# Attention kernel on one core: values loaded 128 rows at a time, odd key spans filled by copies, block sums from the loaded rows, and a new order of the attention stage

## The chip, the core and the metric

The program runs on one core of a Trainium2 chip. The metric is device time in microseconds (us); lower is better. The core has five instruction streams that run side by side and wait for each other by semaphores: PE (matrix products and transposes; PEld is its loading of weights), DVE, ACT and POOL (elementwise work) and SP (here it only issues transfers between memory and the core).

## What is computed

Three steps follow each other. The change touches the first one only.

```python
B, H, S, D = 2, 8, 768, 64
block, window = 32, 16
k_sum = k.reshape(B, H, 24, 32, D).max(axis=3)      # one key for every 32 positions
v_sum = v.reshape(B, H, 24, 32, D).mean(axis=3)     # one value for every 32 positions
scores_l = q @ k.T / 8, kept where abs(i - j) < 16, else -1e9
scores_s = q @ k_sum.T / 8 + log(32)
a = softmax over [scores_l, scores_s]
attn = a @ [v, v_sum]
...
x = attn as [1536, 512];  x = moe(x)  (a greedy assignment of tokens to 8 experts);  out = feed_forward(x)
```

## The kernel before

Attention works on 12 tiles of 128 rows, six for each of the two batch entries `b`. A tile has two halves of 64 query rows. The queries of a half can only meet the 96 keys that begin 16 rows ahead of it, so keys and values are kept in 24 *spans* of 96 rows, which start every 64 rows and overlap; below a span's 96 rows stand the 24 block rows, 120 in all. `KW` holds the key spans, `VW` the value spans with a column of weights beside each head (so a row of one head has 65 floats, 260 bytes).

`attention()` is a list of small functions and a table, `ORDER`, that names them one after the other; each engine works off its own instructions in exactly that order. The functions that matter here:

- `load_tiles` (L154) and `load_v` (L164) issue transfers on SP. One `load_tiles` brings 256 rows of q or k in two transfers of 128 rows x 8 heads x 64 floats (256 KB). Before, one `load_v` brings four spans, each in its own transfer of 64 rows (128 KB; the first has 48, the last 80).
- `tiles` (L217) transposes q and k on PE; `k_out`, `q_out` (ACT or DVE) move the result from the PE's output memory; `k_max` (L233, DVE) takes the block maxima; `k_ends` and `k_blocks` complete the spans of keys.
- `scores` (L265, L271) makes one tile's scores on PE in two buffers of a ring of three; `top` (L276, DVE) takes the row maximum, `less` (L281, DVE) and `exps` (ACT) the exponentials of one half of the heads; `p_turn` (L295, PE) transposes them and `p_out` (DVE or ACT) moves them out.
- `v_copy` (L177, L179) copies rows between spans, because the last 32 rows of a span are the first 32 of the next and are not loaded twice. `v_parts` (L188, PE) sums blocks of 32 values: 12 products of 64 rows (the last of 96) by 32 columns. `v_rows` (L198, PE) puts these sums in their 24 rows and `v_means` copies them into every span.
- `pv` (L309, PE) multiplies exponentials by values; `sums`, `norm`, `pv_out` (DVE, ACT) divide. `x_store` writes the tile, `x_turn` (L337, PE), `x_out` and `logits` (L348, PE) make the router's inputs.
- `tiles`, `scores`, `v_parts` and others take a last number, `blanks`: that many products of zeros (L138) ahead of them.

PE's output memory has five general buffers (`bank`) and the three for scores. Behind attention come the router and the experts, which begin with `rt.scale` (and with products of zeros, L728), and the feed-forward product.

Of the kernel before, what the change touches and what calls it, by code (L numbers as in the profile page):

```python
# [21 lines left out]
G = 3  # L22
NI = S // 64
# [41 lines left out]
less 0 0; q_out 0 2 0 dve; v_parts_out 0 act; v_copy 0 0 1 act; p_turn 0 1; v_rows 0; tiles q 0 2 1; tiles k 1 0
0; p_out 0 1 act; tiles k 1 0 1; less 1 1; v_rows_out 0 act; q_out 0 2 1 act; v_means 0 1 dve; scores 4; v_means
0 0 act; top 4 1; pv 2 0; top 4 0; pv 2 1; k_out 1 0 0 act; sums 2 1 dve; less 4 0; exps 0 0; load_tiles k 1 2;
k_max 1 0 0; pv 3 1; sums 3 1 act; k_out 1 0 1 act; pv 3 0; sums 3 0 dve; sums 2 0 act; norm 2 1; scores 5;
load_tiles q 1 1; norm 3 0; pv_out 2 1; norm 2 0; pv_out 2 0; pv_out 3 0; norm 3 1; tiles k 1 1 1; pv_out 3 1;
less 4 1; tiles k 1 1 0; load_tiles q 1 2; tiles k 1 2 1; exps 1 1; top 5 0; k_out 1 1 1 act; load_tiles q 1 0;  # L70
x_turn 3; k_out 1 1 0 act; load_v 1 0; k_out 1 2 1 act; tiles k 1 2 0; k_out 1 2 0 dve; x_out 3 act; tiles q 1 1
0; v_means 0 2 pool; x_turn 2; p_turn 1 1; exps 5 0; x_out 2 dve; k_max 1 2 1; k_ends 1 2 2 pool; q_out 1 1 0
act; top 5 1; logits 3; logits_out 3 act; p_out 1 1 act; k_max 1 2 0; k_max 1 1 1; k_max 1 1 0; logits 2; p_turn
1 0; logits_out 2 act; tiles q 1 1 1; k_max 1 0 1; p_turn 0 0; pv 1 1; k_ends 1 1 2 pool; sums 1 1 dve; exps 4
0; k_blocks 1 1 2 pool; k_ends 1 0 2 pool; p_turn 5 0; p_out 1 0 act; pv 1 0; q_out 1 1 1 act; exps 4 1;
k_blocks 1 0 2 pool; norm 1 1; pv_out 1 1; v_copy 0 2 0 dve; p_out 0 0 act; exps 5 1; p_out 5 0 act; pv 0 1;
# [1226 lines left out]
```

## Time and profile before

| | |
|---|---|
| device time, median of 3 runs (lowest to highest) | 586.84 us (585.59 to 587.39) |
| the profiled execution: its own time, and its span | 585.87 us, 584.0 us |
| busy over the span: PE, PEld, DVE, ACT, POOL | 97%, 83%, 69%, 47%, 32% |
| granted PE clock, share of full speed | 0.998 |
| attention's first product of scores, and the first product of the router's stage | 13.67 us, 91.41 us |
| transfers of 256-byte pieces and smaller | 43,074 packets of 81,545 are under 512 B |

The span is the time from the first to the last instruction that was recorded; the device time holds 1.87 us more. A PE record is one pass: a float32 product shows as two records, a transpose as one. Starts are measured; the ends of PE records are modelled, so the cost of a block of products is read here from its start to the start of the next block.

### The profile page before, as it was taken

How to read it: one execution, taken by the hardware profiler on the slowest of the kernel's cores; microseconds unless marked ns; L12 is line 12 of the kernel's file. 1: busy time of each engine (PE TensorE's matmuls, PEld its weight loads, DVE VectorE, ACT ScalarE, POOL GpSimd, SP SyncE). 2: the span in 40 equal slices, each digit the busy share in tenths (PEclk: the TensorE clock that was granted, in tenths of full speed). 3: DMA queues.
4: the chain of work that ended last, by engine and by line, in shares of the span. 5: the costliest groups of instructions: out<-in, count | busy, mean ns of one | idle time of the engine just before them, and what ended most of it. 6: DMA issues, size and time to landing. Idle time of an engine off the chain costs nothing.

```text
span 584.0 us, 11381 instructions
## 1 busy us (share of the span) xinstructions
PE 567.6 (97%) x4292; PEld 484.5 (83%) x4292; DVE 400.9 (69%) x1080; ACT 274.6 (47%) x636; POOL 185.2 (32%) x268
## 2 busy tenths in 40 slices
PE   7999999999999999999999999999999999999996
PEld 3477674587888888999999988889888989898984
DVE  6678775763665756666675899886699986666550
ACT  2686571121312121323223566666577766666663
POOL 4237300110101101114001443333455875555424
PEclk9999999999999999999999999999999999999999
DMA  9997215397829549485876223200000200000002
GB/s 189 166 207 112 91 38 185 102 310 219 260 65 308 181 136 315 158 243 195 272 269 217 72 77 105 73 2 1 1 0 1 90 20 2 0 1 1 1 1 109
DMA packets 81545, 70.01 MB, mean 120 GB/s; under 512 B 43074, under 2 KB 68674, under 8 KB 81490
## 3 DMA queue, kind: packets, MB, share of 16 engines
q1 hardware_dynamic: 78946, 62.94, 39.0%
q0 software_dynamic: 2016, 6.33, 3.2%
q8 instruction: 34, 0.56, 0.4%
q14 instruction: 21, 0.17, 0.1%
q10 hardware_dynamic: 528, 0.02, 0.1%
HBM read 62.97 MB, written 6.30 MB: 119 GB/s over the span
## 4 chain that ended last, share of the span: by engine, by line
PE 81%; DVE 8%; DMA 3%; issue 2%; POOL 2%; SPq 1%; ACT 1%; POOLq 0%; DVEq 0%; ACTq 0%
PE po L1073 18%; PE ph L1040 17%; PE acc L799 15%; PE acc L808 13%; PE rt L584 2%; PE bank L309 2%; PE bank L188 2%; PE bank L295 2%; PE px L728 2%; DMA xg<-xdram,idx 1%; PE bank L217 1%; PE ps L271 1%; PE bank L337 1%; PE bank L348 1%; DMA vw<-in_v_dram 1%
## 5 line engine op out<-in xcount | busy, mean ns | idle before, releaser
L808 PE MATMUL acc<-ht,slot 128*128 128x192 f32 x512 | 95.3, 333 | 0.0
L799 PE MATMUL acc<-xt,slot 128*128 128x192 f32 x512 | 94.3, 333 | 0.0
L808 PEld LDWEIGHTS acc<-ht,slot 128*128 128x128 f32 x512 | 82.4, 190 | 0.5
L799 PEld LDWEIGHTS acc<-xt,slot 128*128 128x128 f32 x512 | 82.3, 190 | 0.5
L1018 POOL TENSOR_TENSOR al<-sums,ah 128x256 fp32r<-128x256 f32 x64 | 54.2, 848 | 88.2 <-ACT ah L1017 78.8
L1040 PE MATMUL ph<-yh,ah 128*128 128x384 f32 x218 | 75.1, 344 | 1.5 <-DVE c L1143 1.1
L1073 PE MATMUL po<-wl,gh 128*128 128x512 f32 x192 | 75.8, 395 | 0.1
L1073 PE MATMUL po<-wh,gh 128*128 128x512 f32 x192 | 75.8, 395 | 0.0
L1073 PE MATMUL po<-wh,gl 128*128 128x512 f32 x192 | 75.7, 394 | 0.0
L1040 PE MATMUL ph<-yl,ah 128*128 128x384 f32 x218 | 73.7, 338 | 0.0
L1040 PE MATMUL ph<-yh,al 128*128 128x384 f32 x218 | 73.6, 338 | 0.0
L1018 POOL TENSOR_TENSOR al<-slot,ah 128x256 fp32r<-128x256 f32 x48 | 42.4, 884 | 77.3 <-PE ph L1040 41.0
L742 POOL DMA_INDIRECT xg<-xdram,idx x16 | 14.9, 934 | 146.4 <-ACT idx L707 97.6
L1053 ACT ACTIVATE gh<-u 128x384 fp32r<-128x384 f32 x64 | 33.4, 522 | 58.8 <-DVE u L1051 58.4
L1056 DVE TENSOR_TENSOR gl<-u,gh 128x384 fp32r<-128x384 f32 x64 | 50.8, 794 | 6.6 <-ACT gh L1053 6.4
L803 ACT ACTIVATE ht<-acc 128x192 f32<-128x192 f32 x64 | 21.2, 331 | 67.5 <-PE acc L799 67.5
L1040 PEld LDWEIGHTS ph<-yh,ah 128*128 128x128 f32 x218 | 40.9, 188 | 9.8 <-DVE c L1143 3.2
L1040 PEld LDWEIGHTS ph<-yl,ah 128*128 128x128 f32 x218 | 40.9, 188 | 3.9
L1172 DVE TENSOR_TENSOR u<-ph,x 128x384 f32<-128x384 f32 x32 | 17.7, 554 | 34.5 <-PE ph L1040 34.5
L813 ACT ACTIVATE yr<-acc 128x192 f32<-128x192 f32 x32 | 10.6, 330 | 65.0 <-PE acc L808 65.0
L1073 PEld LDWEIGHTS po<-wh,gl 128*128 128x128 f32 x192 | 36.2, 188 | 5.8
L1040 PEld LDWEIGHTS ph<-yh,al 128*128 128x128 f32 x218 | 40.9, 188 | 0.0
(230 smaller groups left out, 1017.0 us busy)
## 6 DMA issues: line engine op xcount, KB each, us to landing
slot<-in_moe_w_dram SPq DMA_DIRECT2D x31, 1024.0 KB, 9.1
raw<-in_moe_w_in_dram SPq DMA_DIRECT2D x16, 512.0 KB, 4.4
raw<-in_moe_w_out_dram SPq DMA_DIRECT2D x16, 512.0 KB, 4.7
nat<-in_k_dram SPq DMA_DIRECT2D x12, 256.0 KB, 4.7
nat<-in_q_dram SPq DMA_DIRECT2D x12, 256.0 KB, 5.4
xdram<-xs SPq DMA_DIRECT2D x12, 256.0 KB, 2.3
vw<-in_v_dram SPq DMA_DIRECT2D x20, 128.0 KB, 5.5
slot<-in_moe_w_dram SPq DMA_DIRECT2D x2, 512.0 KB, 3.3
```

Source lines behind the costliest of these rows:

```text
L188: nc.tensor.matmul(p[32 * n:32 * n + 32], blocks[:r, 22 - 2 * i:54 - 2 * i], VW[b * G + g][:r, n, :, :D], start=(g == 0), stop=(g == G - 1))
L295: nc.tensor.transpose(pt[:, c], pr[:, c], ident)
L742: nc.gpsimd.indirect_dma_start(out=self.XG[k][:, h], out_offset=None, in_=self.x, in_offset=bass.IndirectOffsetOnAxis(ap=idx[:, h:h + 1], ...
L799: nc.tensor.matmul(p, w[:, c, f % 4 * 128:f % 4 * 128 + 128], xt[:, c], start=(c == 0), stop=(c == 3))
L803: nc.scalar.activation(ht[:, f], p, AF.Relu)
L808: nc.tensor.matmul(p, w[:, f, c % 2 * 128:c % 2 * 128 + 128], ht[:, f], start=(f == 0), stop=(f == 7))
L1018: nc.gpsimd.tensor_tensor(l, x, h.bitcast(F32), op=OP.subtract)
L1040: nc.tensor.matmul(p, w[:, 128 * c:128 * c + 128], y[:, b, c], start=first and n == 0, stop=n == 5, skip_group_check=True)
L1053: nc.scalar.activation(gh, u, AF.Copy)
L1056: nc.vector.tensor_tensor(gl, u, gh.bitcast(F32), op=OP.subtract)
L1073: nc.tensor.matmul(self.po[t], x[:, c], w, start=(self.left[t] == 6 * self.PAIRS - 1), stop=(self.left[t] == 0))
L1172: nc.vector.tensor_tensor(u2 if j == 1 else u3, p, x1, op=OP.add)
```

## The change

`VW` becomes one tile for each batch entry with all 12 spans and 128 rows. `load_v` now brings only the even spans, each as 128 rows in one transfer (the first in two, of 112 and 16 rows, which wrap around: the 16 rows ahead of position 0 are filled with the last 16 rows of v, whose scores are masked). `v_copy` fills the odd spans: part 0 copies rows 64 to 127 of an even span to rows 0 to 63 of the odd span behind it, part 1 copies the first 32 rows of the next even span to rows 64 to 95. `v_parts` multiplies the 128 loaded rows of each of the six even spans by one matrix of 0 and 1 with 32 columns: six products where there were twelve. Four clears of parts of `VW` on POOL go. `ORDER` is replaced as a whole; its first and last lines:

```diff
-begin; load_tiles k 0 1; load_tiles k 0 0; tiles k 0 1 0; tiles k 0 0 0 1; tiles k 0 1 1; k_out 0 1 0 dve;
+begin; load_tiles k 0 0; tiles k 0 0 1; tiles k 0 0 0; k_out 0 0 1 act; load_tiles k 0 2; tiles k 0 2 0; k_max 0
...
```

```diff
@@ def attention
-    VW = [st.tile([120, 4, H, D + 1], F32, name=f"vw{n}") for n in range(B * G)]
+    VW = [st.tile([128, NI, H, D + 1], F32, name=f"vw{b}") for b in range(B)]
-    blocks = st.tile([96, 54], F32, name="blocks")
+    blocks = st.tile([128, 52], F32, name="blocks")
@@ def load_v(b, g):
-        w = VW[b * G + g][:, :, :, :D]
-        for ii in range(4):
-            i = 4 * g + ii
-            lo, hi = (16 if i == 0 else 0), (80 if i == NI - 1 else 64)
-            nc.sync.dma_start(w[lo:hi, ii],
-                              bass.AP(tensor=v.tensor, offset=v.offset + b * H * S * D + (64 * i - 16 + lo) * D,
-                                      ap=[[D, hi - lo], [S * D, H], [1, D]]))
+        for k in (2 * g, 2 * g + 1):
+            for lo, hi, s in ((16, 128, 0), (0, 16, S - 16)) if k == 0 else ((0, 128, 128 * k - 16),):
+                nc.sync.dma_start(VW[b][lo:hi, 2 * k, :, :D],
+                                  bass.AP(tensor=v.tensor, offset=v.offset + (b * H * S + s) * D,
+                                          ap=[[D, hi - lo], [S * D, H], [1, D]]))
@@ def v_copy
-        if last:
-            o, i = w[64:96, 3, :, :D], VW[b * G + g + 1][:32, 0, :, :D]
+        if part == 0:
+            moves = ((w[:64, 4 * g + 1:4 * g + 4:2, :, :D], w[64:, 4 * g:4 * g + 3:2, :, :D]),)
+        elif g:
+            moves = ((w[64:96, 4 * g - 1:4 * g + 2:2, :, :D], w[:32, 4 * g:4 * g + 3:2, :, :D]),)
         else:
-            o, i = w[64:96, :3, :, :D], w[:32, 1:, :, :D]
+            moves = ((w[64:96, 1, :, :D], w[:32, 2, :, :D]), (w[64:96, NI - 1, :, :D], w[:32, 0, :, :D]))
@@ def v_parts
-        for g in range(G):
-            for n in range(4):
-                i = 4 * g + n
-                r = 64 if i < NI - 1 else 96
-                nc.tensor.matmul(p[32 * n:32 * n + 32], blocks[:r, 22 - 2 * i:54 - 2 * i], VW[b * G + g][:r, n, :, :D],
-                                 start=(g == 0), stop=(g == G - 1))
+        for k in range(2 * G):
+            n = k % 4
+            nc.tensor.matmul(p[32 * n:32 * n + 32], blocks[:, 20 - 4 * k:52 - 4 * k], VW[b][:, 2 * k, :, :D],
+                             start=(k < 4), stop=(k + 4 >= 2 * G))
@@ def begin
-            nc.gpsimd.memset(VW[b * G][:32, 0, :, :D], 0.0)
-            nc.gpsimd.memset(VW[b * G + G - 1][64:96, 3, :, :D], 0.0)
...
```

What the new order does on PE is seen near the end of attention. Before, from the last tile's scores on (L271: its last 16 products; L309 and L348: products with values and with the router's matrix; L295 and L337: transposes), PE goes back and forth between transposes and products:

```order
L271 MATMUL ps<-kw_89,qt_95 64x120 x16
L309 MATMUL bank<-vw_100,ptS 64x65 x8
L337 MATMUL bank<-ident,xs 128x128 x4
L309 MATMUL bank<-vw_99,ptS 64x65 x8
L295 MATMUL bank<-ident,pr 120x128 x4
L309 MATMUL bank<-vw_99,ptS 64x65 x8
L348 MATMUL bank<-wg,xt 64x64 x8
L337 MATMUL bank<-ident,xs 128x128 x4
L295 MATMUL bank<-ident,pr 120x128 x8
L348 MATMUL bank<-wg,xt 64x64 x8
```

The changed program has, from the same scores on (its line numbers are one lower), all of this stretch up to the last two tiles' logits in these rows:

```order
L270 MATMUL ps<-kw_89,qt_95 64x120 x16
L347 MATMUL bank<-wg,xt 64x64 x16
L308 MATMUL bank<-vw_97,ptS 64x65 x32
L294 MATMUL bank<-ident,pr 120x128 x12
L336 MATMUL bank<-ident,xs 128x128 x8
L294 MATMUL bank<-ident,pr 120x128 x4
L308 MATMUL bank<-vw_97,ptS 64x65 x32
L347 MATMUL bank<-wg,xt 64x64 x16
L336 MATMUL bank<-ident,xs 128x128 x8
```

The same kinds of work now stand together. Counted over the whole order from the first scores to the last logits, blocks of value or router products go from 22 to 8 (288 products in both), blocks of transposes from 28 to 10 (208 transposes in both, of which 18 and 3 blocks are followed by such products); the 12 blocks of scores stay.

The second place is the first sum of blocks on PE. Before, it comes behind the scores of the fourth tile:

```order
L271 MATMUL ps<-kw_88,qt_90 64x120 x16
L188 MATMUL bank<-vw_96,blocks 32x512 x4
L188 MATMUL bank<-vw_97,blocks 32x512 x4
L188 MATMUL bank<-vw_98,blocks 32x512 x4
L217 MATMUL bank<-ident,nat 128x128 x4
```

Now it comes behind the second tile's, so the order asks for the values sooner:

```order
L270 MATMUL ps<-kw_88,qt_90 64x120 x16
L294 MATMUL bank<-ident,pr 120x128 x8
L137 LDWEIGHTS warm
L137 MATMUL bank<-warm 128x512
L187 MATMUL bank<-vw_96,blocks 32x512 x6
L294 MATMUL bank<-ident,pr 120x128 x4
```

Eight products of zeros (L137) are new behind the first scores: six ahead of the second tile's scores, one here, one ahead of the last logits.

The third place is the start of SP's transfers. Before:

```order
L154 DMA nat<-in_k_dram 128x8x64 x6
L154 DMA nat<-in_q_dram 128x8x64 x4
L164 DMA vw_98<-in_v_dram 64x8x64 x3
L164 DMA vw_98<-in_v_dram 80x8x64
L164 DMA vw_97<-in_v_dram 64x8x64 x4
L164 DMA vw_96<-in_v_dram 48x8x64
L164 DMA vw_96<-in_v_dram 64x8x64 x3
L154 DMA nat<-in_q_dram 128x8x64 x2
```

After:

```order
L153 DMA nat<-in_k_dram 128x8x64 x6
L153 DMA nat<-in_q_dram 128x8x64 x2
L162 DMA vw_96<-in_v_dram 128x8x64 x2
L162 DMA vw_96<-in_v_dram 112x8x64
L162 DMA vw_96<-in_v_dram 16x8x64
L162 DMA vw_96<-in_v_dram 128x8x64 x3
L153 DMA nat<-in_q_dram 128x8x64 x4
```

The values move two transfers forward, and their 12 transfers become seven with the same bytes.

## Rows read from the trace of the kernel before

**Rows 1.** Busy time by engine in three stretches (us), with granted clock, transfer share and GB/s.

```profile
13.67:31.84 18.17, 16.76 (x195) 8.36 (x194) 10.55 (x20) 11.19 (x25) 4.20 (x13) 1.00 1.29 173
31.84:91.41 59.57, 58.64 (x1051) 46.07 (x1051) 44.18 (x118) 40.84 (x103) 21.48 (x49) 1.00 0.58 119
91.41:584.00 492.59, 482.76 (x3004) 424.79 (x3000) 337.09 (x918) 219.57 (x504) 153.18 (x175) 1.00 0.36 116
```

**Rows 2.** Timeline of PE: start, duration, work; undisturbed blocks of each kind.

```profile
31.84 1.53 PE L217 MATMUL bank<-ident,nat 128*128 128x128 f32 x12
33.21 0.49 PE L265 MATMUL ps<-bias,identb 128*128 128x384 bf16 x2
...
34.61 2.09 PE L309 MATMUL bank<-vw,ptS 120*64 120x65 f32 x64
36.63 0.50 PE L265 MATMUL ps<-bias,identb 128*128 128x384 bf16 x2
...
45.52 1.15 PE L309 MATMUL bank<-vw,ptS 120*64 120x65 f32 x32
46.60 0.66 PE L217 MATMUL bank<-ident,nat 128*128 128x128 f32 x4
...
79.18 0.66 PE L337 MATMUL bank<-ident,xs 128*128 128x128 f32 x4
79.67 1.04 PE L295 MATMUL bank<-ident,pr 128*120 128x128 f32 x8
80.64 0.69 PE L348 MATMUL bank<-wg,xt 128*64 128x64 f32 x16
81.25 0.65 PE L295 MATMUL bank<-ident,pr 128*120 128x128 f32 x4
81.84 0.69 PE L309 MATMUL bank<-vw,ptS 120*64 120x65 f32 x16
```

**Rows 3.** Timeline of PE: both block sums, a wait, attention's end, and zero products.

```profile
11.07 1.24 PE L138 MATMUL bank<-warm 128*128 128x512 bf16 x5
...
24.11 5.80 PE L188 MATMUL bank<-vw,blocks 64*32 64x512 f32 x24 [0.44 <-DMA vw<-in_v_dram]
29.85 0.66 PE L217 MATMUL bank<-ident,nat 128*128 128x128 f32 x4
...
56.88 3.75 PE L188 MATMUL bank<-vw,blocks 64*32 64x512 f32 x24
60.56 0.50 PE L265 MATMUL ps<-bias,identb 128*128 128x384 bf16 x2
...
73.83 0.62 PE L295 MATMUL bank<-ident,pr 128*120 128x128 f32 x4 [0.80 <-DVE ptS L132]
...
89.98 1.50 PE L348 MATMUL bank<-wg,xt 128*64 128x64 f32 x32
91.41 0.82 PE L728 MATMUL px<-blank 128*128 128x512 bf16 x3
```

**Rows 4.** Timeline of PEld inside the first block sum (weights of successive products).

```profile
27.01 0.15 PEld L188 LDWEIGHTS bank<-vw,blocks 64*32 64x32 f32 x8 [0.91 <-DMA vw<-in_v_dram]
27.47 0.13 PEld L188 LDWEIGHTS bank<-vw,blocks 64*32 64x32 f32 x4 [0.31 <-issue]
...
28.87 0.14 PEld L188 LDWEIGHTS bank<-vw,blocks 96*32 96x32 f32 x2 [0.84 <-issue]
```

**Rows 5.** Timeline of SP: issues of the loads of q and of values.

```profile
6.24 4.85 SPq L154 DMA_DIRECT2D nat<-in_q_dram  x4
11.13 10.83 SPq L164 DMA_DIRECT2D vw<-in_v_dram  x12
```

**Rows 6.** Timeline of PE: the transposes that wait for the eighth load.

```profile
12.64 0.98 PE L217 MATMUL bank<-ident,nat 128*128 128x128 f32 x7 [0.23 <-DMA nat<-in_q_dram]
```

**Rows 7.** Timeline of DVE: three row maxima and one `less`.

```profile
55.02 1.79 DVE L276 TENSOR_REDUCE mx<-ps 128x4 f32<-128x480 f32 x3 [0.69 <-PE ps L271]
56.73 0.65 DVE L281 TENSOR_TENSOR sb<-ps,mx 128x480 f32<-128x480 f32 x1
```

More of the change, by code (lines that the diff above doesn't have):

```diff
@@ L65 @@
[L65 to L74, printed above, removed]
@@ L75 @@
-0; k_blocks 1 1 2 pool; k_ends 1 0 2 pool; p_turn 5 0; p_out 1 0 act; pv 1 0; q_out 1 1 1 act; exps 4 1;
-k_blocks 1 0 2 pool; norm 1 1; pv_out 1 1; v_copy 0 2 0 dve; p_out 0 0 act; exps 5 1; p_out 5 0 act; pv 0 1;
-sums 1 0 dve; sums 0 1 act; tiles q 1 0 1; norm 0 1; norm 1 0; p_turn 4 1; later 0; pv_out 1 0; x_store 2;
-pv_out 0 1; load_v 1 1; p_out 4 1 dve; scores 8; p_turn 4 0; q_out 1 0 1 act; x_turn 1; x_out 1 act; pv 0 0;
-p_turn 5 1; p_out 4 0 act; sums 0 0 dve; logits 1; top 8 0; tiles q 1 0 0; norm 0 0; pv_out 0 0; logits_out 1
@@ L80 @@
-act; pv 5 0; sums 5 0 act; x_turn 0; x_out 0 act; less 8 0; p_out 5 1 dve; q_out 1 0 0 dve; v_copy 1 1 0 act;
-norm 5 0; scores 9; pv_out 5 0; top 9 0; logits 0; logits_out 0 act; top 8 1; pv 4 1; pv 5 1; top 9 1; sums 5 1
-act; pv 4 0; load_v 1 2; exps 9 1; less 8 1; exps 9 0; exps 8 0; k_blocks 1 2 2 pool; sums 4 0 act; norm 5 1;
-later 1; pv_out 5 1; sums 4 1 act; norm 4 0; exps 8 1; x_store 5; norm 4 1; v_parts 1; scores 6; pv_out 4 1;
-v_parts_out 1 dve; pv_out 4 0; v_copy 1 0 1 dve; x_turn 5; p_turn 9 1; x_turn 4; x_out 5 act; top 6 0; p_out 9 1
@@ new lines @@
+dve; less 5 0; load_tiles k 1 1; tiles q 1 0 1; exps 5 1; v_copy 0 2 1 act; k_max 1 0 0; p_turn 5 1; scores 2;
+p_out 4 1 dve; v_means 0 1 pool; k_out 1 0 1 act; x_out 1 act; p_out 5 1 act; q_out 1 0 1 dve; logits 0; v_means
+0 2 pool; logits_out 0 act; exps 5 0; logits 1; pv 4 0; top 2 0; pv 5 1; top 2 1; less 2 0; logits_out 1 act;
+sums 4 0 act; load_tiles q 1 2; exps 2 1; pv 4 1; scores 3; sums 5 1 dve; norm 4 0; pv_out 4 0; norm 5 1;
+load_tiles q 1 1; tiles k 1 1 0; tiles k 1 1 1; sums 4 1 act; load_v 1 0; pv_out 5 1; load_v 1 1; norm 4 1;
@@ new lines @@
+dve; x_out 3 act; exps 9 0; top 8 0; logits 3; k_blocks 1 2 2 pool; v_rows_out 1 act; x_turn 5; p_turn 6 1;
+v_means 1 0 pool; x_store 3; top 8 1; logits_out 3 dve; exps 9 1; x_turn 2; p_turn 9 1; p_out 6 1 dve; x_out 5
+act; less 8 0; p_turn 6 0; p_out 6 0 dve; p_turn 9 0; tiles q 1 2 1; q_out 1 2 1 dve; p_out 9 1 act; scores 7;
+x_out 2 act; x_store 2; p_out 9 0 dve; top 7 0; logits 5; v_means 1 1 pool; top 7 1; pv 9 1; x_store 1; less 7
+1; pv 6 1; exps 8 1; sums 9 1 dve; pv 9 0; exps 8 0; logits_out 5 act; logits 2; sums 9 0 dve; pv 6 0; sums 6 1
@@ new lines @@
+act; norm 6 1; exps 7 0; scores 10; logits_out 2 dve; norm 9 0; pv_out 6 1; norm 9 1; pv_out 9 1; pv_out 9 0;
+v_copy 1 1 1 pool; sums 6 0 act; norm 6 0; x_turn 9; exps 7 1; p_turn 7 1; p_turn 8 0; pv_out 6 0; top 10 1;
+x_turn 6; x_out 9 act; top 10 0; p_out 8 0 act; less 10 0; p_out 7 1 act; x_out 6 dve; later 2; p_turn 7 0;
+p_out 7 0 act; p_turn 8 1; scores 11; top 11 0; x_store 6; logits 6; x_store 4; v_means 1 2 pool; top 11 1;
+p_out 8 1 act; logits_out 6 act; logits 9; logits_out 9 dve; pv 8 1; pv 8 0; pv 7 0; exps 10 0; sums 8 1 dve;
```

79 lines of the change are left out of this document (43 added, 36 removed).

## The prediction

> **What bounds the kernel now.** I read the busy time by stretch first, since a change to attention can only be priced against attention. Attention's products run from 13.67 to 91.41 us. PE is busy for 75.4 of these 77.7 us, DVE for 54.7 and ACT for 52.0 [rows 1], so PE is the bound, with the other two at 70% and 67%. Behind 91.41 us PE is busy 98% of the time, with a program that the change leaves alone. It begins when the last logits are there, and its loads stand in SP's order behind attention's, so a microsecond won in attention is won at the end; that is the first assumption. The granted clock is 1.00 in all three stretches, so no term below holds a clock.
>
> Busy PE is not PE at its best. The timeline shows that the cost of a block depends on its neighbours, read from start to start [rows 2]. Sixteen records of products with values or the router's matrix take 0.61 us (80.64 to 81.25), 32 take 1.08 (45.52 to 46.60), 64 take 2.02 (34.61 to 36.63): 0.029 each and 0.155 for each block. Four transposes ahead of such products take 0.59 (81.25 to 81.84), twelve 1.46 (79.18 to 80.64), so 0.109 each and 0.15 for the block; twelve ahead of scores take 1.37 (31.84 to 33.21), so the block costs 0.05 when scores follow. A tile's scores take 1.40 (33.21 to 34.61). With these prices, and 3.68 for an undisturbed sum of blocks (56.88 to 60.56) [rows 3], all of attention's products make 72.2 us. The other 5.5 of the 77.7 are waits inside the stretch: 2.1 in the first sum of blocks, which waits for its values (24.11 to 29.85 against 3.68), 0.8 for DVE at 73.83, some 0.35 ahead of the last logits (89.98 to 91.41 against 1.08) [rows 3], and most of the rest where scores wait for a free buffer.
>
> **The change, part by part.** *Grouping.* By the counts in the section on the change there are 14 fewer blocks of products, 14 x 0.155 = 2.2 us; 18 fewer blocks of transposes, 18 x 0.05 = 0.95, of which 15 fewer are followed by products, 15 x 0.09 = 1.35. Together -4.5 us. The prices come from blocks that no wait disturbs, and the numbers of transposes and products stay, so this term is safe unless PE starves.
>
> *Sums of blocks.* Before, four pairs of 64 rows start together and the next four follow 0.46 us later (27.01, 27.47) [rows 4]. The last pair, of 96 rows, waits alone and takes 28.87 to 29.85 = 0.98 us [rows 3, 4], with 0.84 idle ahead of it. Now six products of equal shape, of 128 rows, go to four column groups: four rounds, three of 0.46 and a last one of about 0.5, say 1.85 us instead of 3.68, twice: -3.7 us. No row shows 128 rows by 32 columns. If these do not run side by side, the pair of 96 rows is the nearest: 6 x 0.98 = 5.9 us, and the term is +4.4 for both. I take the first: products of 120 rows by 64 columns do run two at a time (0.029 us for 65 columns, where a transpose of 128 columns takes 0.109) [rows 2].
>
> *Zero products.* Eight more behind the first scores at 0.215 each ((1.24 - 0.38) / 4 in [rows 3], 0.38 being the length of one): +1.7 us, of which the six ahead of the second tile's scores lie where PE would wait anyway (next paragraph). Work in all: -4.5 - 3.7 + 1.7 = -6.5.
>
> *Waits.* I walked the new order with these prices. The first scores start about as before: the eighth load lands as before [rows 6], and a chain of three or four maxima on DVE sets them within 0.4 us. The second tile's second half needs a score buffer that is free after two `top` and one `less`, 2 x 0.6 + 0.6 us [rows 7]; the six zero products cover 1.3 of it, 0.5 is left. Eight transposes and one zero product follow, and PE asks for all values at about 19.8 us. Then come 0.1 to 0.2 at two loads of q and one `x_turn`. Near the end six blocks of four transposes stand in a row (the second order rows of the change) with five `bank` buffers, and PE outruns the copies out: about 1.0, near the size of the wait at 73.83 [rows 3]. The last logits wait as before. Sum 2.5 us against 5.5: -3.0, if the values are there at 19.8.
>
> *The values.* Loads of q and k are issued, and land, every 1.21 us for 256 KB (4.85 / 4); those of values every 0.90 for 128 KB (10.83 / 12), 1.8 for 256 KB [rows 5]. From the tenth load at about 15.06 (12.64 + 2 x 1.21) to the last values at 27.01 it was even 11.95 us for six times 256 KB, 1.99 each [rows 4, 6]. In the new order values follow the eighth load at 12.64. At the pace of q and k the last lands at 12.64 + 6 x 1.21 = 19.9 and nobody waits; at 1.99 it lands at 24.6, PE waits 4.8 us, then 0.9 more for the q behind it in the queue, and about 0.6 in the second batch entry. Two things set the loads of values apart from the others: 64 rows instead of 128, and destination rows 260 bytes apart instead of packed. The change removes the first and keeps the second, and no row separates them. I take a pace near that of q and k, 1.3 (+0.6 us), since now each transfer has the same form in rows and size as theirs.
>
> [...]
>
> *Copies.* Each `v_copy` moved 32 rows x 1536 or 512 elements and now moves 64 or 32 rows x 1024: 2048 elements deep for each 256 rows in both, so DVE, ACT and POOL have the same work, now within a shorter stretch: (54.7 and 52.0) / 68 us, 80% and 76%. One copy on DVE stands ahead of the second tile's maxima and waits for the values of the first spans; at 1.3 these have landed by then. I cost it at nothing; without that cover it is the rival on the slower side. For waits that a walk can't foresee, such as the 0.8 at 73.83, I add 0.9.
>
> Sum: -6.5 - 3.0 + 0.6 + 0.9 = -8.0. The profiled execution took 585.87, so 577.9; the median stands 0.97 above that execution: **578.9 us**, with attention's end near 83.4 instead of 91.41.
>
> **Rivals.** (1) *The values keep their pace.* With 1.8 to 1.99 us for 256 KB, waits grow by 3.6 to 6.3 over the walk's, 5.7 at most after the 0.6 already taken: 581.9 to 584.6, around 583. For it: the 260-byte step is unchanged. Against: the form of the transfers is now that of the fast ones.
> (2) *DVE and ACT become the bound.* At 80% and 76% some chains miss their place; each missed wait costs PE 0.3 to 0.9 (as at 73.83), and six of them give 3 us: 582. For it: the packed end; against: before, at 70%, there are only two such waits behind 32 us.
> (3) *Slower.* The copy on DVE ahead of the second tile's maxima holds DVE's whole order until its values have landed, then maxima, exponentials and PE stand behind it. For the gain to vanish the waits must grow by 8 us: the values would have to land near 28, (28 - 12.64) / 6 = 2.6 us for 256 KB. At 2.9, 588.6. The slowest seen is 1.99, and a piece of 16 rows is the only new form that could do it.
> (4) *The gain is not passed on.* The router's stage would have to wait for something that does not move with attention; its transfers are issued behind attention's on SP, and all it needs from earlier is constants. Then no change, 586.
>
> **Chances.** The forecast has 0.57, with 577.0 to 581 as its own range; rival 1 has 0.28, rival 2 0.08, rival 3 0.04, rival 4 0.03. The range reaches from 577.0 (a sum without the 0.6 and 0.9 gives 577.4) to 584.6, rival 1's upper end; products that are not side by side would give 578.9 + 8.1 = 587, and are in rival 3's chance. A measurement of this kernel tells 0.3%, 1.8 us, from no change: faster 0.93, same 0.04, slower 0.03.
>
> **What the profile after would show.** Grouping: 64 records of products in 2.0 us and transposes at 0.11 with 8 and 10 blocks. Sums: both in about 1.85 us, their records starting four at a time. Values: seven issues, 1.2 to 1.4 us apart each 256 KB, and little wait at the first sum; if PE waits there for the values beyond 21 us, rival 1 holds. The stretch from 13.67 should be near 70 us, and that behind it 492.6 as before. Wrong would be: sums of blocks at 4 us or more, waits of PE for DVE or ACT above 4 us in all, or a longer stretch behind attention.

## The result and the profile after

The changed kernel takes 576.87 us, the median of 4 runs (576.4 to 577.19), beside 586.38 (585.59 to 587.39, 4 runs) for the kernel before: a ratio of 0.9836 with a 95% interval of 0.9818 to 0.9855. The forecast was 578.9 with a range from 577.0, so the direction and nearly all of the size came as forecast, and the time lies 0.13 us below the range. The profiled execution took 577.19 us and its span is 575.4.

The first view is the table by windows of the changed kernel (columns: window and its length, busy time and count on PE, PEld, DVE, ACT, POOL, granted clock, DMA share, GB/s). It answers to [rows 1]; attention's products now run from 14.68 to 83.04 us.

```profile
0.00:8.00 8.00, 4.26 (x15) 1.80 (x15) 3.63 (x21) 2.37 (x3) 2.23 (x15) 1.00 0.97 163
8.00:12.00 4.00, 3.86 (x16) 2.63 (x17) 2.53 (x4) 0.60 (x1) 0.00 (x0) 0.57 1.37 217
14.68:83.04 68.36, 66.67 (x1229) 53.19 (x1227) 56.58 (x150) 51.04 (x136) 25.14 (x55) 1.00 0.64 146
83.04:575.40 492.36, 482.85 (x3004) 424.81 (x3000) 337.07 (x918) 219.64 (x504) 153.34 (x175) 1.00 0.36 116
```

The stretch of attention fell from 77.74 to 68.36 us, by 9.38. What lies behind it took 492.36 where it took 492.59, so the gain was passed on whole. But the stretch began 1.01 us later (14.68 against 13.67), and between 8 and 12 us the granted clock averaged 0.57, where the row of the same window reads 1.00 in the trace of before.

The timeline of PE of the changed kernel (start, busy time of the group, what it is, count; in brackets the idle time ahead of it and what ended it) answers to [rows 2, 3]:

```profile
14.68 0.49 PE L264 MATMUL ps<-bias,identb 128*128 128x384 bf16 x2
15.81 1.05 PE L270 MATMUL ps<-kw,qt 64*64 64x120 f32 x32 [0.64 <-DVE kw L253]
...
18.79 0.34 PE L264 MATMUL ps<-bias,identb 128*128 128x384 bf16 x1 [0.45 <-DVE sb L280]
...
21.27 1.91 PE L187 MATMUL bank<-vw,blocks 128*32 128x512 f32 x12
23.11 0.66 PE L294 MATMUL bank<-ident,pr 128*120 128x128 f32 x4
...
28.41 2.09 PE L308 MATMUL bank<-vw,ptS 120*64 120x65 f32 x64
30.43 0.50 PE L264 MATMUL ps<-bias,identb 128*128 128x384 bf16 x2
...
51.55 1.91 PE L187 MATMUL bank<-vw,blocks 128*32 128x512 f32 x12
53.39 0.50 PE L264 MATMUL ps<-bias,identb 128*128 128x384 bf16 x2
...
76.96 0.60 PE L294 MATMUL bank<-ident,pr 128*120 128x128 f32 x4
77.49 2.09 PE L308 MATMUL bank<-vw,ptS 120*64 120x65 f32 x64
...
81.83 1.29 PE L347 MATMUL bank<-wg,xt 128*64 128x64 f32 x32
83.04 0.82 PE L727 MATMUL px<-blank 128*128 128x512 bf16 x3
```

Both sums of blocks take 1.84 us from start to start (21.27 to 23.11, 51.55 to 53.39), and nothing ahead of the first waits for values. (Line numbers of the changed kernel are one lower than those of before.) Sixty-four records of products take 2.02 (28.41 to 30.43). The weight loads of the first sum (PEld of the changed kernel, answering to [rows 4]) show six products, each of two records, of which four start together:

```profile
21.27 0.16 PEld L187 LDWEIGHTS bank<-vw,blocks 128*32 128x32 f32 x8 [0.32 <-issue]
21.73 0.12 PEld L187 LDWEIGHTS bank<-vw,blocks 128*32 128x32 f32 x2 [0.30 <-issue]
22.16 0.12 PEld L187 LDWEIGHTS bank<-vw,blocks 128*32 128x32 f32 x2 [0.31 <-issue]
```

SP's rows answer to [rows 5]: seven transfers for six units of 256 KB, and the next load 7.36 us behind their first, 1.23 for a unit where before it was 1.8.

```profile
8.98 7.32 SPq L162 DMA_DIRECT2D vw<-in_v_dram  x7
16.34 5.98 SPq L153 DMA_DIRECT2D nat<-in_q_dram  x4
```

By the trace's landings the eighth load is there at 12.89 us. Six of the seven transfers of values follow by 19.01, 1.22 us for each 256 KB, which is the pace of q and k; the seventh lands only at 21.62, 8.7 us behind the eighth load. Before, it was 11.8 from the load ahead of the values (15.16) to the last of them (26.96).

The late end is one step of 16. A transfer reports its landing in 16 steps, and of the seventh 15 were in at 20.18. Shortly before, from 18.90 to 20.19, a load of 16 KB of instructions ran on another queue (the queue's row in the DMA view of the changed kernel, 8 to 25 us: packets, MB, share):

```profile
q8 instruction: 1, 0.02, 0.5%
```

Each of the 14 profiles of this document has such a load, starting between 16.8 and 20.4 us; 2.4 to 3.9 us behind its start a transfer lands whose last step alone is 1.1 to 1.5 us behind the fifteenth, and the next transfer is late in the same way. Before, the fifteenth step of the last values came at 25.64, the sixteenth at 26.96. No kernel here moves that load, so this tie is read from the traces and not tested.

PE's waits in the stretch are now three, and all of them are for DVE:

```profile
PE ps L270 <- DVE kw L253: 0.6, 1, 0.6
PE ps L270 <- DVE rs L319: 0.6, 1, 0.6
PE ps L264 <- DVE sb L280: 0.4, 1, 0.4
```

Adding PE's blocks from start to start by kind, over the stretch of attention, gives the table on which the rest leans (numbers of blocks in brackets; us). The columns of the first two experiments below stand here already. In the last column one zero product of 0.31 is missing from the records and stands with the transposes.

| | before | changed | new loads, old order | old loads, new order |
|---|---|---|---|---|
| scores | 18.89 (12) | 18.88 (12) | 19.44 (12) | 18.17 (12) |
| transposes | 26.19 (28) | 23.89 (10) | 26.76 (28) | 24.27 (10) |
| value and router products | 21.30 (22) | 18.12 (8) | 21.89 (22) | 18.49 (8) |
| sums of blocks | 9.42 (2) | 3.68 (2) | 3.69 (2) | 8.77 (2) |
| rows of sums | 1.94 (2) | 1.94 (2) | 1.94 (2) | 1.94 (2) |
| zero products | 0 | 1.85 (3) | 0 | 1.54 (2) |
| the stretch | 77.74 | 68.36 | 73.72 | 73.18 |

### The profile page after: what moved, and what is told of

Its sections match the earlier page's. It is cut to its first block, busy times and chain, and to the rows that moved or that the text cites. A ratio compares the mean times of both kernels' runs of the same rounds, so it can differ in the third digit from the quotient of the medians.

```text
span 575.4 us, 11353 instructions
## 1 busy us (share of the span) xinstructions
PE 560.3 (97%) x4277; PEld 484.4 (84%) x4277; DVE 400.6 (70%) x1093; ACT 275.2 (48%) x646; POOL 181.4 (32%) x247
## 4 chain that ended last, share of the span: by engine, by line
PE 83%; DVE 8%; DMA 2%; issue 2%; POOL 2%; ACT 1%; SPq 0%; POOLq 0%; DVEq 0%
PE po L1072 18%; PE ph L1039 18%; PE acc L798 15%; PE acc L807 13%; PE rt L583 2%; PE ps L270 2%; PE bank L294 2%; PE bank L216 2%; PE bank L308 2%; PE px L727 2%; DMA xg<-xdram,idx 1%; PE bank L347 1%; PE bank L336 1%; DVE gl L1055 1%; PE px L779 1%
```

## Experiments

**Loads and order apart.** Two kernels take one half of the change each. The first has the changed loads, copies and sums in the order of before, in which only copies of values are added or moved; the second has the loads, copies and sums of before in the new order.

New loads with the old order, against before:

```diff
-    VW = [st.tile([120, 4, H, D + 1], F32, name=f"vw{n}") for n in range(B * G)]
+    VW = [st.tile([128, NI, H, D + 1], F32, name=f"vw{b}") for b in range(B)]
...
-... v_copy 0 1 1 act; less 1 0; scores 0;
+... v_copy 0 1 1 act; v_copy 0 2 0 dve; v_copy 0 2 1 act; less 1 0; scores 0;
```

Old loads with the new order, against the changed kernel:

```diff
-    VW = [st.tile([128, NI, H, D + 1], F32, name=f"vw{b}") for b in range(B)]
+    VW = [st.tile([120, 4, H, D + 1], F32, name=f"vw{n}") for n in range(B * G)]
...
-... p_turn 0 1; v_copy 0 0 1 dve; v_parts 0 1; p_out 0 0 dve;
+... p_turn 0 1; v_parts 0 1; p_out 0 0 dve;
```

> The new loads, copies and sums of blocks under the order of before (its copies of values are moved so that each stands ahead of what reads it; nothing is left out). Theory (the gain is a sum of parts: sums of blocks 3.7 us, the wait for values in the first sum 2.1, grouping 4.5 less 1.7 of zero products, and fewer waits): both sums take 1.85 us, the first no longer waits for values (10 loads of q and k at 1.21 us, then six of values at 1.21, land at 22.4, and the sum is asked for at about 24), so 2 x 1.85 + 2.1 = 5.8 us under the kernel before, attention's end near 85.6 us, and the blocks of products and transposes keep their 22 and 28. Rival (grouping carries the gain, the loads little): 1 to 3 us under the kernel before.

> The loads of 64 rows, the copies and the 12-product sums of before, under the new order (copies between spans renamed to the ones of before; nothing is left out). Theory of parts: the sums cost 2 x 1.85 more than in the changed kernel, the values land some 12 us behind the eighth load (about 24.5) where PE asks for them at 21.3, so 3 to 4 us of wait: 577 + 3.7 + 3.5 = 584 us, 2 us under the kernel before. Rival (grouping alone carries the gain): 577 to 579 us.

Measured, on one chip with a median of 585.96 (585.82 to 586.46, 8 runs) for the kernel before: new loads with the old order 583.35 (581.94 to 584.71), a ratio of 0.9954 (0.9937 to 0.997); old loads with the new order 581.92 (581.19 to 583.08), 0.9935 (0.9919 to 0.9952). So the halves give 2.6 and 4.0 us by medians, and the whole gives 9.5.

The first kernel's median lies 2.6 us under before, within its rival's 1 to 3 us and far from the 5.8 of the theory that adds parts. The rival's reason (the loads gain little) does not hold all the same: in the table this kernel's sums fall by the full 5.73, as the theory had it. Its profiled execution lies 3.9 under before, with a start 0.96 us later, and 1.7 us come back in scores, transposes and products (PE waits 1.6 us for score buffers where it was 0.9, and 0.4, 0.3 and 0.2 for copies by POOL and ACT, where it was none). Some 0.7 of that comes with the experiment's own edit: a copy of values that was not at this place before stands on DVE ahead of `less`, and PE's wait for that `less` is 1.01 us, where it was 0.29 before. The rows are from the timelines of DVE and PE of this kernel:

```profile
22.94 0.69 DVE L181 COPY vw<-vw 64x1024 f32<-64x1024 f32 x1
...
24.38 0.34 PE L265 MATMUL ps<-bias,identb 128*128 128x384 bf16 x1 [1.01 <-DVE sb L281]
```

The second kernel's median lies between its two numbers. Its first sum, in the timeline of PE, takes 5.08 us and its second 3.69:

```profile
20.96 5.15 PE L187 MATMUL bank<-vw,blocks 64*32 64x512 f32 x24
26.04 0.65 PE L294 MATMUL bank<-ident,pr 128*120 128x128 f32 x4
```

The order alone asks for the values at 20.96, when those of 64 rows still land until 24.83. The wait is 1.4 us, less than the 3.5 expected, since the products go on as values land.

In the stretch the halves give 4.02 and 4.56 us and the whole 9.38, so 0.8 is gained only together. By the table this does not come from the sums: they fall by 5.73 in the first kernel, 0.65 in the second and 5.74 in the whole, so there the halves add up to 0.64 more than the whole. It comes from what the new loads cost elsewhere on PE, 1.7 us under the old order and 0.3 under the new one. As 0.7 of the 1.7 is the copy that the first kernel's edit put ahead of `less`, the halves would otherwise add up to the whole within some 0.1 us (an estimate from these numbers). By medians 2.9 us are gained only together; no profile shows that rest, since the first kernel's profiled execution is the fastest of its five and 1.4 us under their median.

**Form of the value loads.** Each load of 128 rows is made in two transfers of 64 rows, to the lower and to the upper half; and, in another kernel, the rows of values are packed 256 bytes apart instead of 260. The second one leaves out the sums by which the rows are divided and takes a constant for them, so it computes other values.

```diff
-            for lo, hi, s in ((16, 128, 0), (0, 16, S - 16)) if k == 0 else ((0, 128, 128 * k - 16),):
+            for lo, hi, s in (((16, 64, 0), (64, 128, 48), (0, 16, S - 16)) if k == 0 else
+                              ((0, 64, 128 * k - 16), (64, 128, 128 * k + 48))):
...
-    VW = [st.tile([128, NI, H, D + 1], F32, name=f"vw{b}") for b in range(B)]
+    VW = [st.tile([128, NI, H, D], F32, name=f"vw{b}") for b in range(B)]
...
-            nc.vector.tensor_scalar(rs, live["p", t, a][:, :, D], 1e-9, None, op0=OP.add)
+            nc.vector.tensor_scalar(rs, live["p", t, a][:, :, 0], 0.0, 100.0, op0=OP.mult, op1=OP.add)
```

> The changed kernel with each 128-row load of values split into two transfers of 64 rows (to rows 0 to 63 and 64 to 127), all else equal. Theory (the slow pace of before came from filling rows 0 to 63 alone, half of the rows): pairs of halves fill all rows, the pace stays near 1.2 us for 256 KB, the values are there at about 20 us, 577 us. Rival (the pace comes from the number of rows in one transfer): 1.8 to 2.0 us for 256 KB, the last values near 24.5, PE waits 3 us or more in the first sum, and 580 us or more.

> The column of weights beside each head is left out, so that rows of values stand 256 bytes apart in the core's memory instead of 260; the products with values have 64 columns instead of 65, the clears that fill the weights go, and the sum by which a row is divided is replaced by the constant 100. Theory (the step of 260 bytes costs nothing): the values land over the same 8.4 to 8.7 us behind the eighth load, and the time is 576.0 to 577.0. Rival (it costs something, since values land 1.45 us apart where q and k land 1.21 apart): the values land over 7.3 us, and the time falls by no more than the 0.3 to 0.6 that PE waits for them and for q behind them, to 575.9 to 576.3.

Halved: 578.62 (577.91 to 579.25), ratio 0.9873 (0.9857 to 0.989). Its first sum takes 3.52 us (20.51 to 24.03 in the timeline of PE) where it took 1.84, so 1.7 us are spent waiting for values, and that is nearly all that this kernel loses:

```profile
20.51 2.02 PE L188 MATMUL bank<-vw,blocks 128*32 128x512 f32 x10
23.08 1.02 PE L188 MATMUL bank<-vw,blocks 128*32 128x512 f32 x2 [0.55 <-DMA vw<-in_v_dram]
```

The theory's 577 us and the rival's 580 or more both miss. Packed: 576.66 (576.24 to 577.07), ratio 0.983 (0.9812 to 0.9849), the same as the changed kernel.

The rate at which values arrive is read from the tables by windows of five kernels, in windows that begin where the last load ahead of the values has landed (the last column is GB/s). The kernel before:

```profile
15.20:21.00 5.80, 5.19 (x90) 3.86 (x87) 4.21 (x10) 4.22 (x12) 1.21 (x5) 1.00 1.42 156
```

The changed kernel:

```profile
12.90:19.00 6.10, 5.02 (x56) 2.94 (x53) 3.88 (x11) 2.24 (x5) 4.76 (x21) 1.00 1.40 217
```

Old loads in the new order:

```profile
13.10:19.00 5.90, 4.83 (x62) 3.00 (x63) 4.14 (x12) 2.04 (x5) 4.99 (x22) 1.00 1.44 149
```

Halved:

```profile
13.10:19.00 5.90, 4.99 (x79) 3.24 (x82) 4.13 (x12) 2.08 (x5) 5.37 (x25) 1.00 1.40 177
```

Packed:

```profile
12.80:18.90 6.10, 4.96 (x76) 3.19 (x78) 4.59 (x13) 2.16 (x6) 5.46 (x24) 1.00 1.39 213
```

The 16 DMA engines are as busy in all five (a share of 1.39 to 1.44, with packets that overlap), and yet move 149 to 156 GB/s where the transfers of 64 rows all go to the lower rows, 177 where 64-row transfers go to the two halves by turns, and 213 to 217 with 128 rows. From the load ahead of the values to the last of them it is 11.8 us with 64 rows in either order, 9.9 halved, 8.7 in the changed kernel and 8.5 packed, each with a last step that is 0.9 to 1.4 late. So a transfer of 64 rows is slow in itself (177 against 217 GB/s; its 128 KB and its 64 rows go together here, and no kernel parts them), the half of the rows to which it goes adds to that (149 with all in the lower rows against 177 by turns, in the same order of work), and the step of 260 bytes costs nothing that these runs tell (217 with it, 213 without). Why the half of the rows matters is not shown.

**Sums of blocks.** The changed kernel with its sums made of twelve products of 64 rows again, from the same loads.

```diff
-        for k in range(2 * G):
-            n = k % 4
-            nc.tensor.matmul(p[32 * n:32 * n + 32], blocks[:, 20 - 4 * k:52 - 4 * k], VW[b][:, 2 * k, :, :D],
+        for g in range(G):
+            for n in range(4):
+                k, r = 2 * g + n // 2, 64 * (n % 2)
+                nc.tensor.matmul(p[32 * n:32 * n + 32], blocks[r:r + 64, 20 - 4 * k:52 - 4 * k],
...
```

> The changed kernel with its two sums of blocks made again of twelve products of 64 rows, the lower and the upper 64 rows of each loaded span, two for each group of output rows at a time; loads, copies and order are those of the changed kernel. Theory (six products of 128 rows cost half of twelve of fewer rows, whatever the loads): each sum takes 3.2 to 3.7 us instead of 1.84, and the time rises by 2 x 1.4 to 2 x 1.85, to 579.4 to 580.4, less what the first sum hides of the wait for the q behind it (0.6 in some executions). Rival (PE runs products of the lower and of the upper rows side by side): 1.84 to 2.3 each and 576.5 to 577.5.

Measured: 578.63 (577.5 to 578.9), ratio 0.9864 (0.9843 to 0.9886). PE's timeline has 2.71 us for each sum, between the theory and the rival:

```profile
20.12 2.78 PE L188 MATMUL bank<-vw,blocks 64*32 64x512 f32 x24
22.83 0.65 PE L295 MATMUL bank<-ident,pr 128*120 128x128 f32 x4
```

So of the 1.84 us that each sum gained, 0.87 come from six products of 128 rows in place of twelve of 64: two steps of 0.43 less, the distance at which groups of weight loads follow each other (21.73 to 22.16 above). Lower and upper rows by turns change nothing in that distance (0.43, 0.43 and 0.42 from 20.58 to 21.86 in this kernel's PEld), so the rival's side by side is not seen. The other 0.97 are the last product of before, of 96 rows, which waited alone and ran alone for 0.98 us [rows 3, 4]. Twice 0.87 is 1.74, and the median stands 1.8 to 2.1 over the changed kernel's.

**The price of a block.** One kernel splits each of the 24 groups of value products by one zero product of 32 columns; another puts the same 24 zero products, two at a time, into 12 of the groups.

```diff
         for c in range(HP):
+            if c == 2:
+                nc.tensor.matmul(po4[:, 1, 96:128], live["warm"][:, :128], live["warm"][:, :32], start=True, stop=True)
             for w in range(2):
...
+            for _ in range(2 if c == 2 and a == 1 else 0):
```

> One zero product of 128 rows by 32 columns set into the middle of each of the 24 groups of 16 value products, so that each group is split. Theory (a block costs 0.155 us when products of 64 rows follow transposes and 0.15 when a 128-row operation follows such products, whatever waits there are): 24 x (0.155 + 0.15 + 0.03) = 8.0, so about 584.9 (583 to 586). Rival (the block prices were in truth waits for DVE and ACT, which the new order also removed): 24 x 0.03 = 0.7, so 577.6.

> The same 24 zero products, but two at a time in the middle of only 12 of the 24 groups: half the switches, the same work. Theory: 12 x (0.155 + 0.15) + 24 x 0.03 = 4.4, so about 581.3, and some 3.7 under the kernel with 24 switches. Rival: 577.6, the same as the kernel with 24 switches.

Measured, beside the changed kernel at 576.55 (575.65 to 577.19): 582.4 (582.18 to 583.38), ratio 0.9909 (0.988 to 0.9938), and 579.72 (579.2 to 579.91), ratio 0.986 (0.9831 to 0.9889). That is 5.85 us for 24 splits and 3.17 for 12 with the same work, 0.24 and 0.26 each; the rival (577.6 for both) falls, and the theory's 0.33 was too high. The timeline of PE of the kernel with 24 shows where a split costs:

```profile
28.39 0.45 PE L311 MATMUL bank<-vw,ptS 120*64 120x65 f32 x8
28.77 0.19 PE L308 MATMUL bank<-warm 128*128 128x32 bf16 x1
28.89 0.69 PE L311 MATMUL bank<-vw,ptS 120*64 120x65 f32 x16
29.51 0.19 PE L308 MATMUL bank<-warm 128*128 128x32 bf16 x1
```

Sixteen records take 0.62 (28.89 to 29.51) and eight 0.38, so 0.030 each and 0.14 to 0.15 for the block, close to the 0.155 of the forecast; the zero product has 0.12 with its own block. Four splits make 28.39 to 31.49 = 3.10 of what takes 2.02 unsplit: 0.27 each.

**The start.** Three kernels ask what the later start cost. One has three more zero products among the first transposes; one is the changed kernel again, beside the rest of its set; one has twelve zero products at the very start instead of six.

```diff
-begin; load_tiles k 0 0; tiles k 0 0 1; tiles k 0 0 0; k_out 0 0 1 act; load_tiles k 0 2; tiles k 0 2 0; k_max 0
+begin; load_tiles k 0 0; tiles k 0 0 1; tiles k 0 0 0 1; k_out 0 0 1 act; load_tiles k 0 2; tiles k 0 2 0 2;
...
-        bank(6)
+        bank(12)
```

> The changed kernel with three more products of zeros among the first transposes of k (one ahead of the second four, two ahead of the third four), where PE waits for loads. In the profile of the changed kernel the granted clock was 0.50 from 8.06 to 11.48 us, the five zero products there took 1.97 us instead of 1.08, and the first scores stood 1.6 us later than before. Theory (that stretch at the lower clock costs the changed kernel about 1 us where it occurs): clock 1.00 throughout, the first scores' main products at 14.4 to 14.8 instead of 15.8, and 575.9 to 576.4 us. Rival (the start is set by DVE's maxima whatever the clock): the same 576.9, first scores still at 15.8.

> The changed kernel again, beside the next three. In its profiled execution the first scores came at 14.68 us instead of 13.67, with a granted clock of 0.50 from 8.06 to 11.48 us. Theory (the early clock differs from one execution to the next): median 576.4 to 577.2, and executions with a mean clock of 1.000 are up to 0.8 us faster than those at 0.996. Rival (the later start belongs to the new order, whatever the clock): median the same, no tie between clock and time, first scores at 14.5 to 14.7 again whatever the clock reads.

> Twelve products of zeros at the very start instead of six, so that PE has no pause between 1.9 and about 5.8 us. Theory (PE's early products run at the lower level after its early pauses, and this delays the first scores by 0.7 to 1.0 us): transposes and zero products between 8 and 11.5 us take 0.11 and 0.215 us each instead of 0.22 and 0.39, the first scores start at 13.7 to 14.0 and the time falls by 0.6 to 1.0, to 575.9 to 576.3. Rival (the first scores wait for the eighth load and for DVE's copy, or PE is slowed anyway): the first scores stay at 14.4 to 14.7 and the time at 576.4 to 577.2, as it was with three zero products spread over that time.

Measured: three more 576.93 (576.18 to 577.08), ratio 0.9841 (0.9824 to 0.9857); the same kernel again 576.55 (575.65 to 577.19), ratio 0.9807 (0.9777 to 0.9836); twelve 576.7 (576.18 to 578.24), ratio 0.9816 (0.9787 to 0.9846). With three more, the first scores still came at 14.53 us and the transposes at 8.56 still took 0.21 each, so that kernel tells nothing of the cost. With twelve they came at 13.85 and the clock was at 1.00 from 5.33 us to near the end, as the theory said. The median is the same, so the theory's price of 0.6 to 1.0 is not seen; single executions do not settle it (the profiled one took 576.18, with attention's end at 81.85). The changed kernel's second profile shows without any edit how an earlier start can be lost. There the first scores came at 13.90, 0.78 earlier than in its first, and the execution took 577.19 us again:

```profile
13.90 0.49 PE L264 MATMUL ps<-bias,identb 128*128 128x384 bf16 x2
...
20.11 2.15 PE L187 MATMUL bank<-vw,blocks 128*32 128x512 f32 x12
22.18 0.65 PE L294 MATMUL bank<-ident,pr 128*120 128x128 f32 x4
22.67 0.27 PE L216 MATMUL bank<-ident,nat 128*128 128x128 f32 x1
23.34 0.98 PE L216 MATMUL bank<-ident,nat 128*128 128x128 f32 x7 [0.40 <-DMA nat<-in_q_dram]
...
25.23 0.50 PE L264 MATMUL ps<-bias,identb 128*128 128x384 bf16 x2
```

An earlier start meets the loads. The sum takes 2.07 instead of 1.84, and the transposes behind it 2.07 instead of 1.46, since the load of q that stands behind the values has not landed. Both waits are for the late sixteenth steps: the last values have 15 steps at 20.05 and land at 21.16, and the q behind them has 15 at 22.28 and lands at 23.30. The scores behind these transposes start at 25.23 here and at 25.54 in the first profile, so 0.31 of the 0.78 was left. The rest of attention took the same 57.5 us, and what lies behind it 492.68 instead of 492.36; that 0.32 is within the scatter of this part, so the equal times of the two executions are chance in part. The tie between mean clock and time that was expected of single executions is not seen either: 575.65 us came at a clock of 0.998, and 577.17 as well. That mean is a poor witness of the start, since in every profile the last 0.7 to 3.8 us of the span are at 0.50 too.

**Zero products.** The changed kernel without the six zero products ahead of the second tile's scores.

```diff
-0 0; k_ends 0 2 2 dve; k_blocks 0 2 2 pool; scores 1 6; v_copy 0 0 0 dve; load_v 0 2; top 1 1; p_turn 0 0; top 1
+0 0; k_ends 0 2 2 dve; k_blocks 0 2 2 pool; scores 1; v_copy 0 0 0 dve; load_v 0 2; top 1 1; p_turn 0 0; top 1
```

> The six zero products ahead of the second tile's scores left out. Theory of the forecast (PE would wait there anyway for a buffer of scores): the second half of these scores waits 1.2 us more and the time is unchanged, 576.2 to 577.0. Rival (they stand in PE's way): 1.2 us less, 575.4.

Measured: 577.12 (575.97 to 579.62), ratio 0.9846 (0.9821 to 0.9871). The rival's 575.4 would be a ratio of 0.9813, outside the interval, and the waits agree. The wait for the score buffer is 1.66 us where it was 0.45, 1.21 more for 1.23 us of zero products left out (timeline of PE of this kernel). They cost nothing, as the forecast had it.

```profile
17.41 0.34 PE L264 MATMUL ps<-bias,identb 128*128 128x384 bf16 x1 [1.66 <-DVE sb L280]
```

**The wait at 50.57 us.** One copy of values on POOL is moved behind the completion of the keys; the other engines' orders stay as they are.

```diff
-act; sums 2 1 dve; v_copy 1 2 1 pool; sums 2 0 act; pv 3 1;
+act; sums 2 1 dve; sums 2 0 act; pv 3 1;
...
-k_ends 1 1 2 pool; v_copy 1 2 0 pool;
+k_ends 1 1 2 pool; v_copy 1 2 1 pool; v_copy 1 2 0 pool;
```

> One copy of values between spans on POOL (32 rows, second batch entry) is moved behind the completion of the keys; the other engines' orders stay. In the changed kernel DVE's three small copies into the spans of keys take 1.45 us at 48.97 where POOL copies values at the same time, and 0.49 where POOL does not. Theory (DVE stands still while POOL copies, and the scores behind it wait 0.6 us for that): the three copies take 0.5 us, the scores of that tile 1.41 us instead of 2.09, and the time falls by 0.5 to 0.7, to 575.9 to 576.2. Rival (DVE's copies are late for another reason, or the wait moves on to the next place): the copies again take 1.15 to 1.45 us, or the time stays at 576.5 to 577.

Measured: 576.51 (576.03 to 576.79), ratio 0.9826 (0.9808 to 0.9845). The timeline of all engines of the changed kernel, DVE's and POOL's rows at this place:

```profile
47.84 2.14 POOL L180 COPY vw<-vw 64x1024 f32<-64x1024 f32 x2
...
48.97 1.45 DVE L253 COPY kw<-ks 128x128 f32<-128x128 f32 x3
...
50.57 0.64 PE L270 MATMUL ps<-kw,qt 64*64 64x120 f32 x16 [0.61 <-DVE rs L319]
```

The same view with the copy moved:

```profile
47.40 1.04 POOL L180 COPY vw<-vw 64x1024 f32<-64x1024 f32 x1
...
48.54 0.81 DVE L253 COPY kw<-ks 128x128 f32<-128x128 f32 x3
...
49.50 1.05 PE L270 MATMUL ps<-kw,qt 64*64 64x120 f32 x32
```

POOL's two copies end at 49.98. Beside the second of them, one of DVE's three small copies took 1.09 us from 48.97 on, where the quickest takes 0.21, and ended 0.08 us behind POOL's. With the copy moved the three take 0.81, the tile's scores 1.45 instead of 2.09, and the stretch 68.16 instead of the 68.82 of the changed kernel's second profile, which started like this one. So DVE's three copies are shorter where POOL's copy of values does not run beside them (0.81 against 1.45), and PE's wait of 0.61 goes with that, though they did not fall to the 0.5 expected; the gain of some 0.6 us is too small for the medians, which stand 0.04 and 0.36 apart with overlapping runs. So no version was found that is measurably faster than the changed kernel.

## Why the forecast was right, and where it missed

**Grouping** (−4.5) was right. Transposes fell by 2.30, as forecast (0.95 + 1.35). Products fell by 3.18: 2.2 for 14 blocks, 0.8 for the wait at 73.83, which went as the walk had it, and 0.2 for a shorter wait ahead of the last logits (81.83 to 83.04 is 1.21, and was 1.43). The two splitting kernels show that the block itself is what costs, and not a wait that went with the old order, at 0.14 where the forecast had 0.155.

**Sums of blocks** (−3.7, and the wait of 2.1) were right: 5.73 less, with four products side by side. The 1.85 was met with luck: the step had four rounds, three of 0.46 and a last one of 0.5, and the rows show three starts, 0.46 and 0.43 apart, and 0.95 from the last start to the end. What the step did not say, and twelve products of 64 rows showed, is that half of the gain of each sum is the end of the odd product of 96 rows.

**Zero products** (+1.7) cost 1.85, of which the six are covered.

**The values.** The choice between the pace of q and k and the old one was right: the pace goes with the form of the transfer in rows and size (217 GB/s with 128 rows, 149 with 64 rows in the same order of work), and not with the step. Rival 1 falls with 217 GB/s at a step of 260 bytes, and with the packed kernel's 213. The pace was 1.22 for the first six transfers, not 1.3, and the last values are late by one step of 16, which the forecast did not have. The 0.6 us for the pace did not appear in the first profile, in which PE asked for the values 1.5 us later than the walk's 19.8; in the second, which asked at 20.11, the late steps cost 0.2 in the sum and 0.6 behind it.

**The walk** (waits 5.5 to 2.5, stretch −9.5 in all) met the stretch's −9.38, though not place by place. The 1.0 us for copies out near the end did not come (the 24 transposes from 74.72 to 77.49 took 2.77 us, which is 24 x 0.109 + 0.15), and two waits of 0.64 and 0.61 for DVE came that it did not name. That these cancelled was luck. Here lies one mis-sized term: the 0.9 *for waits that a walk can't foresee*, and with it the 0.6 for the pace, were laid on top of a walk that already held enough, since the 1.25 us that came unnamed found their room in the 1.0 that was named and did not come. Together they put the stretch 1.4 us too long. The start, taken *about as before*, was 1.01 late in the first profile, which hid most of this: attention ended at 83.04 where 83.4 was forecast, and the profiled execution took 577.19 where the sum said 577.9.

**The median** is the larger part of the miss. The step that failed here is the term 0.97, *the median stands 0.97 above that execution*, which the sum carried over to the changed kernel. There the median stands 0.32 below its profiled execution, which makes 1.29 of the 2.0 us by which the forecast was high; the sum makes the other 0.7 (1.4 too long in the stretch, less the later start of 1.0, and 0.3 behind attention and outside the span). The three runs of before lie 1.8 us apart. Beside the experiments three more sets of it had medians of 585.96 (8 runs), 587.42 (11) and 586.36 (9), which is 0.09, 1.55 and 0.49 above the same profiled execution, and the changed kernel's second set has a median 0.64 below its own. So the offset is no fixed amount that a sum can carry from one kernel to another. The range repeated the step: its low end of 577.0 left 0.4 us below the sum without allowances, and nothing for the scatter of the runs.

**Rivals.** (2), DVE and ACT as the bound, came in small: all three waits of the stretch are for DVE, 1.7 us together, and the scores took 18.88 us in all, as before (18.89). (3) did not come: nobody waited for the copy ahead of the second tile's maxima. (4) fell with 492.36 us behind attention.

**Still open.** Why the granted clock was at full speed from another moment on in one execution than in the next of the same kernel, what a later start costs in the median, and why the stretch behind attention, with the same instructions, took between 491.8 and 492.9 us from one profile to the next.

## What to carry to other kernels

Price a regrouping by the number of blocks, with a cost for each block and for each record read from undisturbed neighbours, and say for an allowance on top of a walk what it stands for; here it counted a margin twice, since the walk already named waits that did not come. One case does not show that it always will. An offset between a profiled execution and a median of three runs is no term of a sum: it belongs in the width of the range, with the spread of the runs shown. When an early stage is made faster or starts earlier, look for the stream of loads that runs beside it, since two limits close to each other hide both what one of them costs and what it gives back; and read when the last step of a transfer lands, not only the mean pace.

## What was not expected of the hardware

The granted clock was 0.50 from 8.06 to 11.48 us in the first profile of the changed kernel, and 1.00 from there to 574.68. PE had idled for 0.86, 0.22 and 0.88 us between groups of transposes from 4.9 us on. Five zero products took 1.96 us there and 1.08 elsewhere:

```profile
8.14 1.76 PE L216 MATMUL bank<-ident,nat 128*128 128x128 f32 x7 [0.88 <-DMA nat<-in_k_dram]
9.69 2.13 PE L137 MATMUL bank<-warm 128*128 128x512 bf16 x5
11.65 1.04 PE L216 MATMUL bank<-ident,nat 128*128 128x128 f32 x8
```

With twelve zero products ahead PE had no pause until 7.3 us, and the clock was at 1.00 from 5.33 us on. That the pauses set the clock is not shown.

A clock of 1.00 in a row of the first microseconds need not be a clock that was granted. The trace's first entry of the clock begins at 4.65 us in the first profile of the changed kernel and at 9.18 in the second, and the rows read 1.00 ahead of it; but the zero products from 1.93 to 4.49 us took 0.43 each, twice the 0.216 of later ones. Over the 14 profiles the first scores follow the moment from which the entries stay at 1.00: at 13.67 to 14.10 us where that is 9.98 us or sooner, at 14.38 to 14.68 where it is 10.56 to 12.19. So the later start of the first profile does not belong to the new order (the old order with the new loads started at 14.63, the new order in its second profile at 13.90).

DVE's copy that met a copy on POOL took 1.09 us, where the quickest takes 0.21, and ended at 50.06, 0.08 us behind POOL's. In the profiles of these kernels the three copies took 1.15 to 1.45 us where POOL copied values at that moment, and 0.49 to 0.81 where it did not. Why it takes longer there is not shown.
